# Three small edits in a decayed-attention and two-MLP kernel: two adds and a memset go from GpSimd to VectorE, and one set of sums of squares comes later

## The chip, the core and the metric

The kernel runs on one core of a Trainium2 chip. The core has five engines with in-order queues of their own: TensorE (PE, with weight loads shown as PEld), VectorE (DVE), ScalarE (ACT), GpSimd (POOL) and SyncE (SP, which here issues most DMAs). The metric is the device time of one launch in microseconds (us). Three runs of the kernel before took 890.89, 891.45 and 895.48 us; their median is 891.45 us.

## The reference

Three stages, in float32, on 4 sequences of 576 tokens with 8 heads of 64:

```python
scores = scale * q @ k.T                       # per head, 576 x 576
decay  = cum[:, :, :, None] - cum[:, :, None, :]   # cum = cumsum(log(clip(f)))
attn   = softmax(where(causal, -1e9, scores + decay))
x      = attn @ v                              # back to (4, 576, 512)
# first MLP, with LayerNorm and a residual
xn = (x - mean) / sqrt(var + 1e-6) * g_ln
x  = x + relu(xn @ w_ch1) @ w_ch2              # 512 -> 2048 -> 512
# gated MLP: h = relu(x @ w_in); u, v = halves; v is normalised over its features,
# mixed over the tokens by w_spatial, times u, then @ w_out
```

Two steps of it matter below: the variance of LayerNorm (a mean of squares over 512 features), and the softmax, whose rows are multiplied with v.

## The kernel before, in words

**Staging.** The attention is cut into eight blocks of query rows (`BLOCKS`): blocks 0 and 1 are rows 0 to 127 of two sequences each, blocks 2 and 3 rows 128 to 255 of two sequences each, blocks 4 to 7 rows 256 to 575 of one sequence each. What is left over of the last four (64 rows each) forms a ninth block of the first MLP. When a block's attention is done, its 256 tokens go through `norm`, and then form a group of the first MLP (`mlp`, 16 slices of the hidden layer). While PE works on the MLP of one group, the attention of a later block fills in: a table of due times in `run` (`SPAN`, `BEGIN`, and the constants `QKL`, `QKS`, `QKN` for `qknorm`) sets in which order the pieces are written, and a scheduler then orders each engine's queue from that.

**Arithmetic.** Products in full float32 are made from pairs of float16 halves: a high half made on ACT (`copy`, L304, or L669 for the weights) and a low half made on DVE (L388, L672). `make16` (L664 ff) makes the halves of the first MLP's weights once their scale is known.

**norm (L685 ff).** A tile x of 128 partitions by 4 x 256 tokens holds 512 features. PE takes the mean with a matrix of ones (L682); DVE subtracts it (L696); ACT squares (`sq`, L699); the four quarters of `sq` are folded to one by two adds on GpSimd (L703: 128 x 512, L704: 128 x 256); PE takes the mean of the result (L682 again); ACT and DVE make 1/sqrt of it (L707 to L711). Blocks 7 and 8 don't fold: PE sums the four quarters itself. So the fold occurs seven times, for blocks 0 to 6.

**GpSimd's other work.** For blocks 4 to 7 `operands` broadcasts rows of decays over the partitions (L338, a custom instruction, 96 times in all) and masks them (L342). In `weights` (L345 ff) a tile P of probabilities is cut into halves; for the last query tile, which has 64 columns less, its last columns are cleared by GpSimd (L382, 16 times) before P is transposed by DMA (L391) for the product with v (`values`, L533). P's buffers are a ring of five, so a clearing waits until the transposes of the same tile of the pair of heads before have been read out.

**qknorm (L260 ff).** q and k are scaled by powers of two that come from their sums of squares. Eight tiles of 896 KB are loaded through GpSimd's DMA queue (L277) into four buffers; for each, DVE sums the squares of q (L284) and ACT those of k (L285). The results set a scale (L290 to L297), then GpSimd scales the rows of decays and writes them to DRAM (L298, L299), where `operands` of block 4 reads them (L323).

Of the kernel before, what the change touches and what calls it, by code (L numbers as in the profile page):

```python
# [13 lines left out]
AF = mybir.ActivationFunctionType  # L14
ALU = mybir.AluOpType
# [21 lines left out]
NARROW = 4  # L37
# [29 lines left out]
F64_LO = 2.0 ** -15  # L67
VS = 10

QKL, QKS, QKN = 0.98, 1.2, 0.02  # L70
QKB = 4
MID = 416
CMAX = 2.0 ** 15
# [19 lines left out]
class Kernel:  # L93
# [166 lines left out]
    def qknorm(self):  # L260

        nc, W, C = self.nc, QW, QW + S
        n = B * NP // 2
        cm = self.pool("qs")
        qs = cm.__enter__()
        ss = self.cst.tile([P, 2, n], F32, name="qkss")
        tot = self.cst.tile([P, 2], F32, name="qkt")
        sm = self.qksc = self.cst.tile([P, 2, 2], F32, name="qksc")
        one = self.cst.tile([P, 1], F32, name="qkone")
        self.qkneg = self.cst.tile([P, 1], F32, name="qkneg")  # L270
        tiles = []

        def load():
            i = len(tiles)
            tiles.append(qs.tile([P, 2, C], F32, tag="qs", name="qs", bufs=QKB))
            b, p = i * 2 // NP, i * 2 % NP
            nc.gpsimd.dma_start(out=tiles[i], in_=self.pair_of(b)[p : p + 2].rearrange("p r s -> r p s"))  # L277

        for i in range(QKB):
            load()  # L280
        yield
        for i in range(n):
            q, k = tiles[i][:, :, :W], tiles[i][:, :, W:]
            nc.vector.tensor_tensor_reduce(out=q, in0=q, in1=q, scale=1.0, scalar=0.0, op0=ALU.mult, op1=ALU.add, accum_out=ss[:, 0, i : i + 1])  # L284
            nc.scalar.activation(k, k, AF.Square, accum_out=ss[:, 1, i : i + 1])  # L285
            if len(tiles) < n:
                load()
            yield
        nc.vector.tensor_reduce(out=tot, in_=ss, axis=mybir.AxisListType.X, op=ALU.add)
        pn = self.bank("s")  # L290
        nc.tensor.matmul(pn[:, :2], lhsT=self.ones, rhs=tot, start=True, stop=True)
        self.pow2(pn[:, :2], sm, up=3, k=0)
        uq, uk, sq, sk = (sm[:, i, j : j + 1] for i in range(2) for j in range(2))
        nc.vector.tensor_scalar(out=sk, in0=uq, scalar1=CMAX, scalar2=sk, op0=ALU.mult, op1=ALU.min)
        nc.vector.tensor_scalar(out=uk, in0=sq, scalar1=1.0 / CMAX, scalar2=uk, op0=ALU.mult, op1=ALU.max)
        nc.vector.tensor_scalar(out=one, in0=sq, scalar1=sk, scalar2=None, op0=ALU.mult)
        nc.vector.tensor_scalar(out=self.qkneg, in0=uq, scalar1=uk, scalar2=-0.125, op0=ALU.mult, op1=ALU.mult)  # L297
        nc.gpsimd.tensor_scalar(out=self.drow, in0=self.drow, scalar1=one[: B * H], scalar2=1.0, op0=ALU.mult, op1=ALU.mult)  # L298
        nc.gpsimd.dma_start(out=self.decay_d, in_=self.drow)  # L299
        cm.__exit__(None, None, None)  # L300
# [44 lines left out]
    def weights(self, i, heads):  # L345

        nc, at, bufs, q0 = self.nc, self.at, BUFS, 2 * P
        lo, hi = qtile(i)
        R, N, nb, qs = hi - lo, hi, i + 1, slice(lo - q0, hi - q0)
# [5 lines left out]
        for job in jobs:  # L355
            for g, (x, y) in enumerate(((xl, xh), (xh, xl), (xh, xh))):
                for u, n in job:
                    us, (c0, c1) = slice(64 * u, 64 * u + 64), cuts[n if R < P else 0]
                    out = banks[n][us if R < P else slice(0, P), : c1 - c0]
                    ins = nc.tensor.matmul(out, lhsT=x[us, qs], rhs=y[us, QW + c0 : QW + c1], start=g == 0, stop=g == 2, skip_group_check=True)  # L360
# [6 lines left out]
        for w in range(1 if R < P else 2):  # L367
            sd = at.tile([P, S], F32, tag="sd", name="sd", bufs=bufs["sd"])
            st = at.tile([P, 5], F32, tag="st", name="st", bufs=bufs["st"])
            for n, (c0, c1) in enumerate(cuts):  # L370
                self.marks["seen"] = nc.vector.tensor_tensor_reduce(  # L371
                    out=sd[:, c0:c1], in0=banks[n if R < P else w][:, : c1 - c0], in1=decay[i, w][:, c0:c1], scale=self.qkneg,
                    scalar=3e38 if n == 0 else st[:, n - 1 : n], op0=ALU.add, op1=ALU.min, accum_out=st[:, n : n + 1])
            n = len(cuts) - 1
            nc.scalar.activation(sd[:, :N], sd[:, :N], AF.Exp, bias=st[:, n : n + 1], scale=-1.0, accum_out=st[:, 2:3])  # L375
            rs = st[:, 3:4]
            nc.scalar.activation(rs, st[:, 2:3], AF.Copy, bias=1e-9 / SC, scale=1.0 / SC)  # L377
            nc.vector.reciprocal(rs, rs)  # L378
            ph = at.tile([P, 5, 2, P], F16, tag="P16", name="P16", bufs=bufs["P16"])
            pieces = [(0, i), (i, nb)] if R < P else [(0, nb)]  # L380
            if R < P:
                nc.gpsimd.memset(ph[:, i, :, R:], 0.0)  # L382
            for k0, k1 in pieces:
                wd = P if k1 * P <= N else R
                src = sd[:, k0 * P : k0 * P + (k1 - k0 - 1) * P + wd].rearrange("p (t w) -> p t w", w=wd)
                dh, dl = ph[:, k0:k1, 0, :wd], ph[:, k0:k1, 1, :wd]
                self.copy(0, dh, src, rs)
                low = nc.vector.scalar_tensor_tensor(out=dl, in0=src, scalar=rs, in1=dh, op0=ALU.mult, op1=ALU.subtract)  # L388
            for u in range(2) if R < P else [w]:
                rows = slice(R * u, R * u + R) if R < P else slice(0, P)  # L390
                tr = nc.sync.dma_start_transpose(out=heads[u][1][:, : 2 * nb, qs], in_=ph[rows, :nb].rearrange("p t h w -> p (t h w)"))  # L391
                self.in_order("tr", tr)
            if w == 0 and R == P:
                yield
# [269 lines left out]
    def make16(self, j):  # L664

        nc, src = self.nc, self.wt[:, j + 2]
        h, l = self.pair(j)
        for c, sc in ((slice(0, DM), self.w1c[:, 1]), (slice(DM, 2 * DM), self.w2c[:, 1])):
            ins = nc.scalar.activation(h[:, c], src[:, c], AF.Copy, scale=sc)  # L669
            if j >= SOON:  # L670
                self.after(ins, self.xh)
            nc.vector.scalar_tensor_tensor(out=l[:, c], in0=src[:, c], scalar=sc, in1=h[:, c], op0=ALU.mult, op1=ALU.subtract)  # L672

    def pair(self, j):
        w = self.wt[:, j].bitcast(F16)
# [6 lines left out]
            self.nc.tensor.matmul(pm, lhsT=self.onesf, rhs=x, start=i == 0, stop=i == len(xs) - 1)  # L682
        return pm

    def norm(self, x, s, y, whole, end, c):  # L685


        nc, ns = self.nc, self.ns
# [11 lines left out]
        if s is None or end:  # L700
            pv = self.mean(tag, *(sq[:, t] for t in range(NK)))
        else:
            nc.gpsimd.tensor_tensor(out=sq[:, :2], in0=sq[:, :2], in1=sq[:, 2:], op=ALU.add)  # L703
            nc.gpsimd.tensor_tensor(out=sq[:, 0], in0=sq[:, 0], in1=sq[:, 1], op=ALU.add)  # L704
            pv = self.mean(tag, sq[:, 0])
        t1 = ns.tile([P, TOK], F32, tag="t1", name="t1", bufs=2)
        nc.scalar.activation(y, pv, AF.Ln, bias=self.eps)  # L707
# [379 lines left out]
    def run(self):  # L1087
        self.setup()
        last = len(BLOCKS)
# [37 lines left out]
        def prep(n):  # L1127
# [22 lines left out]
            if g == 0:  # L1150
                self.y0 = y
            xc = tile() if n == 0 else xT
            g = self.norm(xT, s, y, g > 0, n >= last - 1, xc)
            while True:
                try:
                    with self.tc.high_priority(1):
# [169 lines left out]
```

## Time and profile before

| What | Value |
|---|---|
| median of three runs | 891.45 us (890.89 to 895.48) |
| the profiled execution: its time, its span | 894.41 us, 892.7 us |
| PE busy | 778.0 us (87% of the span) |
| DVE busy | 558.0 us (63%) |
| ACT busy | 513.0 us (57%) |
| POOL busy | 176.3 us (20%) |
| mean granted clock of TensorE | 0.933 of full speed |

The time of the profiled execution is that of the device; its span is what lies between the first and last instruction of the trace, here 1.7 us less. "Busy" counts instructions that work; an engine's idle time is put down to the event that ended it. A PE that is busy is not always at its full clock: the granted clock tells at which of its levels it ran.

### The profile page before, as it was taken

How to read it: one execution, taken by the hardware profiler on the slowest of the kernel's cores; microseconds unless marked ns; L12 is line 12 of the kernel's file. 1: busy time of each engine (PE TensorE's matmuls, PEld its weight loads, DVE VectorE, ACT ScalarE, POOL GpSimd, SP SyncE). 2: the span in 40 equal slices, each digit the busy share in tenths (PEclk: the TensorE clock that was granted, in tenths of full speed). 3: DMA queues.
4: the chain of work that ended last, by engine and by line, in shares of the span. 5: the costliest groups of instructions: out<-in, count | busy, mean ns of one | idle time of the engine just before them, and what ended most of it. 6: DMA issues, size and time to landing. Idle time of an engine off the chain costs nothing.

```text
span 892.7 us, 16774 instructions
## 1 busy us (share of the span) xinstructions
PE 778.0 (87%) x6108; PEld 574.9 (64%) x6108; DVE 558.0 (63%) x1481; ACT 513.0 (57%) x1294; POOL 176.3 (20%) x288
## 2 busy tenths in 40 slices
PE   8799988999647992899299749999999989999998
PEld 7588876877435771567187537784444757867776
DVE  4798599585536772877197728468843476273644
ACT  4878599584525762667176617446732583555643
POOL 2100011002526541534165223001002100000000
PEclk7999997999968997899699959999999989999999
DMA  8789794487414882577168707465203322010101
GB/s 249 220 307 332 237 300 78 73 168 124 121 45 98 145 164 48 96 138 162 28 120 174 127 19 108 96 200 144 93 1 65 73 66 76 1 55 1 47 8 54
DMA packets 162840, 103.99 MB, mean 116 GB/s; under 512 B 105955, under 2 KB 151139, under 8 KB 162757
## 3 DMA queue, kind: packets, MB, share of 16 engines
q1 hardware_dynamic: 155352, 88.91, 41.4%
q0 software_dynamic: 6400, 12.23, 6.7%
q10 hardware_dynamic: 1004, 1.78, 0.7%
q8 instruction: 48, 0.79, 0.4%
q14 instruction: 36, 0.29, 0.1%
HBM read 63.99 MB, written 14.72 MB: 88 GB/s over the span
## 4 chain that ended last, share of the span: by engine, by line
PE 47%; DVE 19%; issue 12%; ACT 10%; DMA 9%; POOL 3%; SPq 1%; POOLq 0%; DVEq 0%; ACTq 0%
PE ph L779 8%; PE acc L764 7%; PE pb L719 7%; PE pb L720 7%; PE pb L721 7%; DVE sd L371 3%; DMA PT<-P 2%; ACT sd L375 2%; DVE P L388 2%; ACT P L304 2%; DMA raw<-in_moe_w_ch_dram 2%; POOL D L338 2%; PE av L533 2%; DVE xql L328 2%; DVE hl L790 1%
## 5 line engine op out<-in xcount | busy, mean ns | idle before, releaser
L764 PE MATMUL acc<-hh,wt 128*128 128x256 f16 (+2 forms) x960 | 200.3, 298 | 4.3 <-DVE t L809 4.1
L779 PE MATMUL ph<-xh,wt 128*128 128x256 f16 (+1 forms) x896 | 192.0, 295 | 2.9 <-DVE hl L790 1.8
L779 PEld LDWEIGHTS <-wt 128*128 128x128 f16 x1344 | 132.0, 100 | 55.5 <-issue 16.3
L764 PEld LDWEIGHTS <-wt 128*128 128x128 f16 x1344 | 130.8, 99 | 53.6 <-issue 10.6
L779 PE MATMUL ph<-xl,wt 128*128 128x256 f16 (+1 forms) x448 | 132.2, 295 | 3.7 <-DVE xl L741 3.7
L764 PE MATMUL acc<-hl,wt 128*128 128x256 f16 (+1 forms) x416 | 117.4, 285 | 0.6 <-DVE hl L790 0.6
L338 POOL PARTITION_BROADCAST D<-row x96 | 81.9, 895 | 124.2 <-DVE st L371 66.7
L304 ACT ACTIVATE P<-sd,st 128x384 f16<-128x384 f32 (+2 forms) x128 | 70.0, 586 | 21.9 <-DVE st L378 16.0
L375 ACT ACTIVATE sd<-sd,st 128x384 f32<-128x384 f32 (+2 forms) x80 | 54.8, 685 | 46.7 <-DVE st L371 46.5
L786 ACT ACTIVATE hh<-ph 128x256 f16<-128x256 f32 (+2 forms) x128 | 50.7, 398 | 46.4 <-PE ph L779 46.1
L790 DVE SCALAR_TENSOR_TENSOR hl<-ph,hh 128x256 f16<-128x256 f32 (+1 forms) x112 | 50.6, 456 | 34.1 <-ACT hh L786 32.7
L682 PE MATMUL av<-sq,onesf 128*128 128x256 f32 x14 | 6.8, 578 | 74.5 <-POOL sq L704 74.5
L388 DVE SCALAR_TENSOR_TENSOR P<-sd,st,P 128x512 f16<-128x512 f32 (+1 forms) x96 | 60.3, 656 | 17.9 <-ACT P L304 16.8
L811 POOL DMA_DIRECT2D x_d<-t x36 | 33.6, 1116 | 147.0 <-DVE t L807 117.8
L378 DVE RECIPROCAL st<-st 128x1 f32<-128x1 f32 x80 | 11.7, 156 | 73.5 <-ACT st L377 73.5
L371 DVE CUSTOM_DVE_ANT_0 sd<-s,D,qkneg 128x384 f32<-128x384 f32 (+2 forms) x80 | 49.7, 644 | 12.6 <-PE s L360 12.1
L682 PEld LDWEIGHTS av<-sq,onesf 128*128 128x128 f32 x14 | 3.1, 258 | 76.1 <-POOL sq L704 76.0
L533 PE MATMUL av<-PT,vp 128*64 128x320 f16 (+2 forms) x480 | 35.8, 286 | 13.7 <-DMA PT<-P 13.2
L533 PEld LDWEIGHTS <-vp 128*64 128x64 f16 (+1 forms) x480 | 27.0, 115 | 24.1 <-issue 13.6
L719 PE MATMUL pb<-x2h,wil 128*128 128x288 f16 (+2 forms) x144 | 37.8, 273 | 0.0
L720 PE MATMUL pb<-x2l,wih 128*128 128x288 f16 (+2 forms) x144 | 37.8, 273 | 0.0
L721 PE MATMUL pb<-x2h,wih 128*128 128x288 f16 (+2 forms) x144 | 37.8, 273 | 0.0
(296 smaller groups left out, 1778.3 us busy)
## 6 DMA issues: line engine op xcount, KB each, us to landing
raw<-in_moe_w_ch_dram SPq DMA_DIRECT2D x32, 512.0 KB
qs<-in_qk_dram POOLq DMA_DIRECT2D x8, 896.0 KB, 9.2
qk<-in_qk_dram SPq DMA_DIRECT2D x16, 448.0 KB
vraw<-in_v_dram SPq DMA_DIRECT2D x5, 1024.0 KB
vr<-in_v_dram SPq DMA_DIRECT2D x16, 320.0 KB
x_d<-xT SPq DMA_DIRECT2D x9, 512.0 KB
x_d<-t POOLq DMA_DIRECT2D x36, 128.0 KB, 4.4
out_dram<-o SPq DMA_DIRECT2D x32, 144.0 KB
```

Of the source, the lines that this page charges most:

```text
L304: self.nc.scalar.activation(out, in_, AF.Copy, scale=scale)
L338: gp.partition_broadcast(t if R == P or u else t[:R], row[32 * u : 32 * u + 1, :hi], channels=P if R == P or u else R)
L371: self.marks["seen"] = nc.vector.tensor_tensor_reduce(out=sd[:, c0:c1], in0=banks[n if R < P else w][:, : c1 - c0], in1=decay[i, w][:, c0: ...
L375: nc.scalar.activation(sd[:, :N], sd[:, :N], AF.Exp, bias=st[:, n : n + 1], scale=-1.0, accum_out=st[:, 2:3])
L388: low = nc.vector.scalar_tensor_tensor(out=dl, in0=src, scalar=rs, in1=dh, op0=ALU.mult, op1=ALU.subtract)
L533: ins = nc.tensor.matmul(pav[us, n0:W], lhsT=vp[:kr, vi, kt, us], rhs=heads[u][1][:kr, 2 * kt + pi, n0:W], start=(kt == 0 and (vi, pi) == ...
L719: first = mm(out, lhsT=al, rhs=bh, start=start, stop=False, **kw)
L720: mm(out, lhsT=ah, rhs=bl, start=False, stop=False, **kw)
L721: mm(out, lhsT=ah, rhs=bh, start=False, stop=stop, **kw)
L764: ins = nc.tensor.matmul(acc[m], lhsT=a, rhs=b, start=bank not in clear, stop=last and e == len(terms) - 1, skip_group_check=True)
L779: ins = nc.tensor.matmul(ph, lhsT=a, rhs=b, start=k == e == 0, stop=k == NK - 1 and e == len(terms) - 1)
L790: nc.vector.scalar_tensor_tensor(out=hl, in0=ph, scalar=0.0, in1=hh, op0=ALU.max, op1=ALU.subtract)
```

## The change

Three edits:

1. `norm` gets an argument that names the engine of the fold. For blocks 0, 1 and 2 it stays GpSimd; for blocks 3 to 6 it is VectorE.
2. The clearing of P's last columns (`ph[:, i, :, R:]`) is done on VectorE.
3. `QKS`, the due time from which the sums of squares of q and k are written, goes from 1.2 to 1.325, and their spacing `QKN` from 0.02 to 0.008; both instructions of each tile are ordered behind the last low half that `make16` makes (`self.marks["made"]`). `after` gives an order of the schedule and no wait of its own.

```diff
-QKL, QKS, QKN = 0.98, 1.2, 0.02
+QKL, QKS, QKN = 0.98, 1.325, 0.008
...
-            nc.vector.tensor_tensor_reduce(out=q, in0=q, in1=q, ..., accum_out=ss[:, 0, i : i + 1])
-            nc.scalar.activation(k, k, AF.Square, accum_out=ss[:, 1, i : i + 1])
+            for ins in (nc.vector.tensor_tensor_reduce(out=q, in0=q, in1=q, ..., accum_out=ss[:, 0, i : i + 1]),
+                        nc.scalar.activation(k, k, AF.Square, accum_out=ss[:, 1, i : i + 1])):
+                self.after(ins, self.marks["made"])
...
-                nc.gpsimd.memset(ph[:, i, :, R:], 0.0)
+                nc.vector.memset(ph[:, i, :, R:], 0.0)
...
-            nc.vector.scalar_tensor_tensor(out=l[:, c], in0=src[:, c], scalar=sc, in1=h[:, c], ...)
+            self.marks["made"] = nc.vector.scalar_tensor_tensor(out=l[:, c], in0=src[:, c], scalar=sc, in1=h[:, c], ...)
...
-            nc.gpsimd.tensor_tensor(out=sq[:, :2], in0=sq[:, :2], in1=sq[:, 2:], op=ALU.add)
-            nc.gpsimd.tensor_tensor(out=sq[:, 0], in0=sq[:, 0], in1=sq[:, 1], op=ALU.add)
+            fold.tensor_tensor(out=sq[:, :2], in0=sq[:, :2], in1=sq[:, 2:], op=ALU.add)
+            fold.tensor_tensor(out=sq[:, 0], in0=sq[:, 0], in1=sq[:, 1], op=ALU.add)
...
-            g = self.norm(xT, s, y, g > 0, n >= last - 1, xc)
+            g = self.norm(xT, s, y, g > 0, n >= last - 1, xc, self.nc.gpsimd if n < NARROW - 1 else self.nc.vector)
```

How this moves instructions is shown at three places. From L282 on, line numbers of the changed kernel are higher by one.

On GpSimd, at the fold of block 4 (`sq` is the tile of squares, `D` the broadcast decays, `row` their source; an `ISA` without a tile asks for another set of GpSimd code). Before:

```order
L342 AFFINE_SELECT D_4064<-D_4064 64x64 x2
L703 ISA
L703 TENSOR_TENSOR sq_3615<-sq_3615 128x512
L338 ISA
L338 ISA D_4356<-row_4345 128x384
L338 ISA D_4354<-row_4345 128x384
L704 ISA
L704 TENSOR_TENSOR sq_3615<-sq_3615 128x256
L342 AFFINE_SELECT D_4356<-D_4356 128x128
L342 AFFINE_SELECT D_4354<-D_4354 128x128
L338 ISA
L338 ISA D_4366<-row_4345 128x512
```

and now:

```order
L343 AFFINE_SELECT D_4064<-D_4064 64x64 x2
L339 ISA D_4356<-row_4345 128x384
L339 ISA D_4354<-row_4345 128x384
L343 AFFINE_SELECT D_4356<-D_4356 128x128
L343 AFFINE_SELECT D_4354<-D_4354 128x128
```

The two adds, the clearing (which stood some rows further down) and the four changes of code around the adds are gone from GpSimd's queue; from the first broadcast on, only broadcasts, masks and DMAs stand there.

On VectorE, at the same place (`s` are scores in PSUM, `st` row statistics, `hl` a low half of the hidden layer, `P` the probabilities; `ISA` rows of L371 are the biased minimum and the read of its result). Before:

```order
L696 TENSOR_TENSOR xT<-xT,av 128x256 x4
L388 SCALAR_TENSOR_TENSOR P_3935<-sd,st,P_3935 128x4x128
L388 SCALAR_TENSOR_TENSOR P_3935<-sd,st,P_3935 128x64
L371 ISA sd,st<-s_3976,D,qkneg 128x384
L371 ISA st 128x1
L371 ISA sd,st<-s,D,qkneg 128x384
L371 ISA st 128x1
L790 SCALAR_TENSOR_TENSOR hl<-ph,hh 128x256
L378 RECIPROCAL st<-st 128x1 x2
L388 SCALAR_TENSOR_TENSOR P_3990<-sd,st,P_3990 128x3x128
```

and now:

```order
L697 TENSOR_TENSOR xT<-xT,av 128x256 x4
L389 SCALAR_TENSOR_TENSOR P_3935<-sd,st,P_3935 128x4x128
L372 ISA sd,st<-s_3976,D,qkneg 128x384
L372 ISA st 128x1
L389 SCALAR_TENSOR_TENSOR P_3935<-sd,st,P_3935 128x64
L372 ISA sd,st<-s,D,qkneg 128x384
L372 ISA st 128x1
L791 SCALAR_TENSOR_TENSOR hl<-ph,hh 128x256
L704 TENSOR_TENSOR sq<-sq 128x512
L379 RECIPROCAL st<-st 128x1
L705 TENSOR_TENSOR sq<-sq 128x256
L791 SCALAR_TENSOR_TENSOR hl<-ph,hh 128x256
```

Between the subtraction of the mean (L697) and the first add stand six rows of other work; the second add follows the first with one reciprocal in between.

On ScalarE, at the squares of k (`qs` is a loaded tile, `wt` the weights' halves, `hh` the ReLU of the MLP, `vp` halves of v). Before, first rows of the stretch:

```order
L669 ACTIVATE wt<-wt,w2c 128x512
L285 ACTIVATE qs,qkss<-qs 128x2x576
L217 ACTIVATE vp,vq<-vr 128x256
L699 ACTIVATE sq<-xT 128x1024
L285 ACTIVATE qs,qkss<-qs 128x2x576
L669 ACTIVATE wt<-wt,w1c 128x512
L669 ACTIVATE wt<-wt,w2c 128x512
L786 ACTIVATE hh<-ph 128x256
L285 ACTIVATE qs,qkss<-qs 128x2x576
```

and now:

```order
L670 ACTIVATE wt<-wt,w1c 128x512
L670 ACTIVATE wt<-wt,w2c 128x512
L507 ACTIVATE xT<-av,vs 128x128
L217 ACTIVATE vp,vq<-vr 128x256
L285 ACTIVATE qs,qkss<-qs 128x2x576 x4
L787 ACTIVATE hh<-ph 128x256
L488 ACTIVATE sd,st<-sd,st 128x256 x2
L787 ACTIVATE hh<-ph 128x256
```

The squares stood between the weights' halves; now four of them stand in one run behind the last of these halves, and the other four follow one at a time between the ReLUs and softmax pieces of blocks 2 and 3.

## Rows read from the trace of the kernel before

**Rows 1.** The page's 40 slices of 22.3 us, busy tenths of PE.
```profile
PE   8799988999647992899299749999999989999998
```

**Rows 2.** Waits of PE: for what, us in total, times, longest.
```profile
PE av L682 <- POOL sq L704: 74.5, 5, 20.8
PE av L533 <- DMA PT<-P: 13.2, 11, 4.0
```

**Rows 3.** PE in order of time: start, us, operation, [idle before, releaser].
```profile
258.35 1.22 PE L682 MATMUL av<-sq,onesf 128*128 128x256 f32 x2 [20.81 <-POOL sq L704]
...
356.54 1.22 PE L682 MATMUL av<-sq,onesf 128*128 128x256 f32 x2 [17.79 <-POOL sq L704]
...
442.98 1.22 PE L682 MATMUL av<-sq,onesf 128*128 128x256 f32 x2 [17.09 <-POOL sq L704]
...
526.03 1.22 PE L682 MATMUL av<-sq,onesf 128*128 128x256 f32 x2 [17.69 <-POOL sq L704]
```

**Rows 4.** Busy us by stretch: length, PE, PEld, DVE, ACT, POOL, clock, DMA, GB/s.
```profile
132.50:137.60 5.10, 1.01 (x19) 0.81 (x16) 5.10 (x15) 5.10 (x12) 0.01 (x1) 0.80 0.00 1
137.60:145.50 7.90, 7.89 (x41) 5.79 (x42) 7.90 (x23) 7.90 (x22) 3.62 (x4) 0.50 0.79 113
...
258.30:262.00 3.70, 3.65 (x16) 2.58 (x17) 1.57 (x4) 1.77 (x5) 0.00 (x0) 0.53 0.01 2
356.50:361.00 4.50, 4.46 (x19) 3.04 (x19) 1.67 (x4) 2.47 (x6) 0.50 (x2) 0.52 0.02 4
443.00:446.30 3.30, 3.30 (x14) 2.30 (x15) 0.92 (x2) 1.53 (x5) 0.43 (x2) 0.53 0.00 0
...
511.00:526.00 15.00, 0.00 (x0) 0.00 (x0) 0.34 (x1) 0.00 (x0) 2.07 (x5) 0.50 0.02 4
526.00:531.50 5.50, 5.47 (x25) 3.60 (x27) 1.25 (x3) 2.09 (x5) 0.48 (x2) 0.50 0.20 38
```

**Rows 5.** POOL in order of time, around the fold of block 4.
```profile
340.25 1.26 POOL L703 TENSOR_TENSOR sq<-sq 128x512 f32<-128x512 f32 x1 [7.93 <-DVE st L371]
347.31 1.23 POOL L338 PARTITION_BROADCAST D<-row  x2 [5.80 <-issue]
355.78 0.71 POOL L704 TENSOR_TENSOR sq<-sq 128x256 f32<-128x256 f32 x1 [7.24 <-issue]
...
362.88 1.95 POOL L338 PARTITION_BROADCAST D<-row  x2 [5.88 <-DVE st L371]
```

**Rows 6.** ACT in order of time, the squares of block 4.
```profile
334.14 1.06 ACT L699 ACTIVATE sq<-xT 128x1024 f32<-128x1024 f32 x1 [1.38 <-DVE xT L696]
```

**Rows 7.** DVE in order of time, during the fold of block 1.
```profile
110.83 0.75 DVE L672 SCALAR_TENSOR_TENSOR wt<-wt,w1c 128x512 f16<-128x512 f32 x1
111.49 1.77 DVE L672 SCALAR_TENSOR_TENSOR wt<-wt,w2c 128x512 f16<-128x512 f32 x1
```

**Rows 8.** POOL in order of time, the first add of block 1.
```profile
111.14 1.57 POOL L703 TENSOR_TENSOR sq<-sq 128x512 f32<-128x512 f32 x1 [0.31 <-ACT sq L699]
```

**Rows 9.** Groups of instructions by line: busy us, mean ns of one, idle before.
```profile
L285 ACT ACTIVATE qs<-qs 128x1152 f32<-128x1152 f32 x8 | 9.2, 1150 | 0.0
L284 DVE CUSTOM_DVE_ANT_1 qs<-qs 128x640 f32<-128x640 f32 x8 | 7.4, 919 | 0.0
...
L254 DVE TENSOR_TENSOR vtr<-vgram,ident 128x512 f32<-128x512 f32 x1 | 0.7, 683 | 0.0
```

**Rows 10.** Line L382, the clearing: ns min/median/max; its engine's idle time before it.
```profile
L382 POOL MEMSET P<- x16: 196/204/532, 265.9 to 560.0; 128x128 f16 x16
...
  DMA PT<-P: 8.6, 2
```

**Rows 11.** Line L277, the loads of q and k: time from issue to landing.
```profile
DMA to landing us min/median/max: 6.7/9.2/10.6
```

**Rows 12.** POOL in order of time, the write of the scaled decays.
```profile
204.93 0.84 POOL L299 DMA_DIRECT2D decay_d<-drow  x1
```

**Rows 13.** SP's queue in order of time, block 4's first reads of the decays.
```profile
220.37 0.73 SPq L323 DMA_DIRECT2D row<-decay_d  x2
```

More of the change, by code (lines that the diff above doesn't have):

```diff
@@ L283, in qknorm @@
             q, k = tiles[i][:, :, :W], tiles[i][:, :, W:]
-            nc.vector.tensor_tensor_reduce(out=q, in0=q, in1=q, scale=1.0, scalar=0.0, op0=ALU.mult, op1=ALU.add, accum_out=ss[:, 0, i : i + 1])
-            nc.scalar.activation(k, k, AF.Square, accum_out=ss[:, 1, i : i + 1])
+            for ins in (nc.vector.tensor_tensor_reduce(out=q, in0=q, in1=q, scale=1.0, scalar=0.0, op0=ALU.mult, op1=ALU.add, accum_out=ss[:, 0, i : i + 1]),
+                        nc.scalar.activation(k, k, AF.Square, accum_out=ss[:, 1, i : i + 1])):
+                self.after(ins, self.marks["made"])
             if len(tiles) < n:
@@ L671, in make16 @@
                 self.after(ins, self.xh)
-            nc.vector.scalar_tensor_tensor(out=l[:, c], in0=src[:, c], scalar=sc, in1=h[:, c], op0=ALU.mult, op1=ALU.subtract)
+            self.marks["made"] = nc.vector.scalar_tensor_tensor(out=l[:, c], in0=src[:, c], scalar=sc, in1=h[:, c], op0=ALU.mult, op1=ALU.subtract)
     def pair(self, j):
@@ L683, in mean, with norm @@
         return pm
-    def norm(self, x, s, y, whole, end, c):
+    def norm(self, x, s, y, whole, end, c, fold):
         nc, ns = self.nc, self.ns
```

## The prediction

> **What bounds the kernel now.** I read four views, from coarse to fine. First the page's slices: PE works at 9 tenths nearly everywhere, but slices 11, 15, 19 and 23 (counted from 0) show 4, 2, 2 and 4 [rows 1]. Four holes at a distance of some 85 us, which is one block of attention: something happens once per block. Then the waits of PE: 74.5 us of idle time are put down to one line, the second mean of `norm`, released by GpSimd's second add of the fold; the next largest wait, on transposes of P, is 13.2 us in eleven pieces [rows 2]. The timeline of PE gives the four large ones, at blocks 3 to 6: 20.81, 17.79, 17.09 and 17.69 us, together 73.4 us [rows 3]. Third, what the other engines do then: in 511 to 526 PE and ACT do nothing, DVE 0.34 us, the DMA engines are at 0.02, and GpSimd itself is busy for only 2.07 of 15 us [rows 4]. So nothing is prefetched or caught up on in a hole; the whole kernel stands still, and it stands for something that is not even GpSimd's work.
>
> What that is, GpSimd's timeline tells. At block 4 the squares were ready at 334.14 + 1.06 = 335.2 [rows 6], PE came to the mean at 356.54 - 17.79 = 338.75 [rows 3]. The first add started at 340.25; between it and the second GpSimd did two broadcasts, and in front of each of these pieces it sat 5.8 to 7.2 us with no releaser but "issue" [rows 5]. The adds and the broadcasts alternate, and each alternation is where the order shows a bare `ISA` row, a change of GpSimd's code. The adds themselves take 1.26 and 0.71 us; three changes of some 5 to 7 us each make up the 21 us from the squares to the folded tile. A fourth change, back to the broadcasts, costs another 5.88 us before 362.88 [rows 5], when PE already runs again.
>
> **The change, part by part. The fold.** It removes from GpSimd the two adds of blocks 3 to 6 and with them all sixteen changes of code; the four waits of 73.4 us lose their cause [rows 3]. It adds the same two adds to DVE. No 128x512 add of two SBUF tiles on DVE stands in the trace, but one from PSUM and SBUF does: 0.68 us [rows 9]; the second is half as long, and I take 0.4. What is late next? At block 4 the squares come at 335.2, and PE needs the fold at 338.75: 3.55 us of cover. In DVE's new order a ReLU low half, and perhaps the last of two score passes, stand ahead of the first add and a reciprocal between the adds; that leaves the fold done 2 to 4 us after the squares, so PE waits 0 to 0.5 us, and I put 2 us in all for the four blocks. Upper bound: 5 us for each, 20 us, if the add always comes behind a full pass of scores and low halves. Gain 71.4.
>
> A word against it. While GpSimd's first add ran from 111.14 to 112.71 [rows 8], a two-input DVE instruction of L672 that takes 0.75 us took 1.77 [rows 7]: the two engines slowed each other. The Trainium skill ("GPSIMD Engine Reference", section 1, Specifications) says that GpSimd shares its SBUF interfaces with VectorE and that DVE instructions with two SBUF inputs contend there. The moved adds have two SBUF inputs, and broadcasts run beside them all the time; by this rule each pair of adds would cost some 1.5 us more, an estimate, 6 us in four blocks. By the rows alone it is 0 to that, as no broadcast beside an add on DVE is seen, and the bound of 20 us holds it.
>
> **The clock.** After each hole PE runs at half of its full clock: the granted clock is 0.50 to 0.53, which is the 1.2 GHz level, in the four stretches behind them, with 3.65, 4.46, 3.30 and 5.47 us of PE work [rows 4], 16.9 us in all. At the 2.4 GHz level that is 8.4 us. PE stood idle before each of these stretches and would not any more. Some of it is work that ran ahead of DVE and ACT catching up; I take 6, with 0 and 8.4 as bounds.
>
> **The clearing.** Sixteen memsets of 0.2 us leave GpSimd [rows 10]; on DVE I take 0.1 us each, 1.6 us of an engine that is 63% busy, hidden by PE's work. It now carries a wait in DVE's queue: for the transposes of the same tile one pair of heads before. Behind it stand the low halves of P of the third query tile and the next scores, for whose transposes PE waits. On GpSimd this wait showed in 2 of 16 cases, 8.6 us together [rows 10]. But `values` on PE waits for the same transposes at about the same time [rows 2], so most of a hold is time that PE doesn't have anyway. I take a loss of 1, bounds 0 and 8.6.
>
> **The squares of q and k.** 8 x 0.92 = 7.4 us of DVE and 8 x 1.15 = 9.2 us of ACT [rows 9] leave the stretch from 103 to 140, where both engines are busy all the time: 5.10 of 5.10 us, while PE works 1.01 [rows 4]. There PE waits 4.1 us for the output copies of group 0, which stand behind squares and weights' halves in DVE's queue; then follow 7.89 us at clock 0.50 [rows 4], 3.9 us lost by that. Ideal gain 8; since ACT and DVE still have the halves to make, I take 4. The bill comes later: four squares in one run hold ACT for 4 x 1.15 = 4.6 us in front of a ReLU that PE needs two hidden slices later, and the last four need loads that go out only when a buffer is free and land 6.7 to 10.6 us later [rows 11]. In between lies about as much other ACT work. I take a loss of 2, bounds 0 and 10. Two queues are moved past: on GpSimd the loads now stand behind the output adds of group 0, and the scaled decays are written behind the four output adds of group 1, some 3.5 us later than at 204.93 [rows 12]; their reader starts at 220.37 [rows 13], 15 us after, and covers it. So net gain 2, bounds -10 and +8.
>
> **The sum.** 73.4 - 2 + 6 - 1 + 4 - 2 = 78.4 us. The profiled execution took 894.4 us (its span 892.7 and 1.7 around it): 816.0. It was 3.0 us above the median of the three runs, so the median after should be 891.45 - 78.4 = 813.
>
> **The rivals.** *The wait moves to DVE (A).* The fold now stands in the queue of an engine that is full in the attention of these blocks, and each mean still waits 5 us; the clock then drops all the same. Gain 73.4 - 20 + 2 = 55: 836. For it: an in-order queue with score passes of two at a time. Against: the order puts the adds early, and 3.55 us of cover. *More comes back (B).* The broadcasts that came late after a hole made `values` wait for transposes: the longest such wait, 4.0 us, and much of the 13.2 [rows 2], would go as well, with the whole of the clock's 8.4 and 8 for the squares: 73.4 + 8.4 + 8 + 5 = 95: 797. *The squares collide (C).* ACT holds for each late load, PE's ReLU is behind it: the loss is 10 and the gain there 0: 73.4 - 2 + 6 - 1 - 10 = 66: 825. *Slower (D).* The clearing holds DVE each time until the transposes are out, as it did on GpSimd twice. If each of 16 took 8.6 us, that is 138 us: 813 + 138 = 951; from 78.4 / 16 = 4.9 us each on the change loses. Against: 14 of 16 had no wait [rows 10] on an engine that comes to them no later than DVE will. *It doesn't do what it says (E).* Other GpSimd work could still ask for the old code between the broadcasts, and the holes would stay: 890. Against: the new order has no bare `ISA` row after the first, and masks and clearings ran between broadcasts without one before.
>
> **How the numbers follow.** Forecast 0.70, A 0.11, B 0.08, C 0.07, D 0.02, E 0.02. The forecast's own range is 803 to 825. The range that should hold 8 in 10 reaches to B below and to A above: 799 to 836. A change below 0.5% (4.5 us) can't be told from none here: faster 0.96, same 0.02, slower 0.02.
>
> **What would show it.** Right: no wait of PE on GpSimd's adds beyond the first microseconds of the kernel; no slices of 2 to 4 before the end of the attention; the mean's matmuls released by DVE with waits below 1 us; clock near 1.0 through the blocks; GpSimd without idle "issue" pieces of 6 us; the squares behind the last weights' halves and PE's wait near 133 shorter. Wrong: waits of some 5 us at the four means on DVE (A); ACT idle for a load near 155 to 165 (C); DVE idle for transposes ahead of memsets (D); the four holes still there (E).

## The result: 816 us, and the profile after

The changed kernel takes 815.71 us (median of 4 runs, 812.2 to 817.82), the kernel before beside it 891.17: a ratio of 0.914, 95% interval 0.9094 to 0.9186. In a second set of runs, reported at the end of the experiments, the ratio was 0.9157 (0.9132 to 0.9181). The profiled execution took 812.2 us, its span 810.5; it is the fastest of its four, as that of before was near its slowest, so the two spans differ by 82.2 us and the medians by 75.5. One execution of a kernel further down, the one without the squares, took 979.22 us at a mean granted clock of 0.747, where its six others took 813.7 to 819.3, and nothing is read from it.

The page's slices, PE's busy tenths, against [rows 1]:

```profile
PE   8799998997899899899899989999999899999998
```

The four slices of 2 and 4 are gone; what is left below 8 is a 7 in slices 1 and 9. PE is busy 764.6 us instead of 778.0 and idle 45.9 instead of 114.7. The waits of PE (what for, us in total, times, longest), against [rows 2]:

```profile
PE av L534 <- DMA PT<-P: 9.9, 11, 2.1
PE ph L780 <- DVE hl L791: 8.9, 8, 1.7
PE s L481 <- DMA qk<-decay_d: 2.4, 1, 2.4
PE ph L780 <- ACT xh L741: 2.0, 1, 2.0
```

The 74.5 us on GpSimd's second add have become 1.1, one wait in the first microseconds. The four matmuls of the mean at blocks 3 to 6, in order of time (start, us, operation, [idle before, releaser]), against [rows 3]:

```profile
230.19 0.60 PE L683 MATMUL av<-sq,onesf 128*128 128x256 f32 x2
310.62 0.60 PE L683 MATMUL av<-sq,onesf 128*128 128x256 f32 x2
375.37 0.60 PE L683 MATMUL av<-sq,onesf 128*128 128x256 f32 x2
438.55 0.67 PE L683 MATMUL av<-sq,onesf 128*128 128x256 f32 x2 [0.55 <-ACT st L378]
```

Three of them wait for nothing, and the fourth 0.55 us for something else than the fold. A pair takes 0.60 us where it took 1.22: the clock. Stretches behind these four means, as long as those of [rows 4] (length, PE, PEld, DVE, ACT, POOL, granted clock, DMA share, GB/s):

```profile
230.20:234.20 4.00, 4.00 (x40) 3.13 (x39) 3.40 (x7) 3.03 (x8) 3.78 (x9) 1.00 0.24 63
310.60:315.10 4.50, 4.50 (x45) 3.57 (x44) 2.87 (x10) 3.56 (x11) 2.07 (x4) 1.00 0.66 114
375.30:378.60 3.30, 3.30 (x34) 2.69 (x33) 2.44 (x7) 2.42 (x8) 1.88 (x3) 1.00 1.13 107
438.50:444.00 5.50, 5.45 (x48) 4.43 (x48) 5.21 (x15) 4.75 (x12) 1.75 (x4) 1.00 0.47 87
```

All at 1.00, the 2.4 GHz level. GpSimd around the fold of block 4, which is [rows 5] with the adds gone:

```profile
301.02 2.29 POOL L339 PARTITION_BROADCAST D<-row  x2 [4.10 <-DVE st L372]
303.39 0.79 POOL L343 TENSOR_SCALAR_AFFINE_SELECT D<-D 64x64 f32<-64x64 f32 x2
306.86 1.40 POOL L339 PARTITION_BROADCAST D<-row  x2 [2.68 <-DVE st L372]
308.33 0.94 POOL L343 TENSOR_SCALAR_AFFINE_SELECT D<-D 128x128 f32<-128x128 f32 x2
```

No piece of idle "issue" stands between them; GpSimd waits for buffers that VectorE gives free. A change of code (a bare `ISA` row of the order) stands in the trace as two records named MODIFY_POOL_CONFIG. At the line of the broadcasts there were 18 in the kernel before, two changes to the broadcasts' code for each of the four folds and one ahead of the first broadcast, and 8 at each line of the adds; in the changed kernel only the first pair is left (ns min/median/max, first and last start):

```profile
L338 POOLq MODIFY_POOL_CONFIG  x18: 1/1/358, 209.2 to 526.7; - x18
...
L339 POOLq MODIFY_POOL_CONFIG  x2: 42/42/42, 206.8 to 206.8; - x2
```

On ScalarE and VectorE the same fold reads (two adds of later blocks below it):

```profile
305.59 1.06 ACT L700 ACTIVATE sq<-xT 128x1024 f32<-128x1024 f32 x1
```

```profile
307.69 0.98 DVE L704 TENSOR_TENSOR sq<-sq 128x512 f32<-128x512 f32 x1
308.70 0.42 DVE L705 TENSOR_TENSOR sq<-sq 128x256 f32<-128x256 f32 x1
...
373.06 0.68 DVE L704 TENSOR_TENSOR sq<-sq 128x512 f32<-128x512 f32 x1
...
436.90 0.71 DVE L704 TENSOR_TENSOR sq<-sq 128x512 f32<-128x512 f32 x1
```

From the end of the squares (306.65) to the folded tile (309.12) it is 2.5 us, where it was 21. And line L383, the clearing, now on VectorE (ns min/median/max, first and last start; its engine's idle time before it), against [rows 10]:

```profile
L383 DVE MEMSET P<- x16: 112/112/112, 235.8 to 486.3; 128x64 uint32 x16
...
  DMA PT<-P: 1.0, 3
```

### The profile page after: what moved, and what is told of

Read it like the earlier page. It is cut to its first block, busy times and chain, and to the rows that moved or that the text cites. A ratio compares the mean times of both kernels' runs of the same rounds, so it can differ in the third digit from the quotient of the medians.

```text
span 810.5 us, 16721 instructions
## 1 busy us (share of the span) xinstructions
PE 764.6 (94%) x6108; PEld 568.1 (70%) x6108; DVE 561.8 (69%) x1505; ACT 509.7 (63%) x1294; POOL 174.1 (21%) x264
## 4 chain that ended last, share of the span: by engine, by line
PE 65%; DVE 15%; DMA 8%; ACT 7%; issue 4%; SPq 1%; DVEq 0%; ACTq 0%
PE ph L780 15%; PE acc L765 13%; PE pb L720 7%; PE pb L721 7%; PE pb L722 7%; DMA PT<-P 4%; PE av L534 3%; PE s L765 3%; DVE sd L372 2%; DVE xql L329 2%; ACT P L305 2%; DVE P L389 2%; ACT sd L376 1%; PE s L361 1%; DVE vp L226 1%
## 5 line engine op out<-in xcount | busy, mean ns | idle before, releaser
L765 PE MATMUL acc<-hh,wt 128*128 128x256 f16 (+2 forms) x960 | 197.3, 296 | 1.7 <-DVE t L808 1.4
L780 PE MATMUL ph<-xh,wt 128*128 128x256 f16 (+1 forms) x896 | 186.5, 290 | 11.0 <-DVE hl L791 8.9
L780 PEld LDWEIGHTS <-wt 128*128 128x128 f16 x1344 | 129.6, 99 | 61.9 <-issue 25.5
L765 PEld LDWEIGHTS <-wt 128*128 128x128 f16 x1344 | 129.6, 98 | 47.1 <-issue 8.6
L780 PE MATMUL ph<-xl,wt 128*128 128x256 f16 (+1 forms) x448 | 130.0, 290 | 0.0
L339 POOL PARTITION_BROADCAST D<-row x96 | 84.1, 917 | 116.0 <-DVE st L372 95.6
L534 PE MATMUL av<-PT,vp 128*64 128x320 f16 (+2 forms) x480 | 33.3, 270 | 9.9 <-DMA PT<-P 9.9
L1063 DVE SCALAR_TENSOR_TENSOR u<-pb,wsc,u 128x288 f32<-128x288 f32 x32 | 15.9, 515 | 34.3 <-PE pb L1062 34.3
L343 POOL TENSOR_SCALAR_AFFINE_SELECT D<-D 128x128 f32<-128x128 f32 (+1 forms) x96 | 36.8, 397 | 4.7
L534 PEld LDWEIGHTS <-vp 128*64 128x64 f16 (+1 forms) x480 | 24.7, 109 | 17.7 <-issue 8.4
L720 PE MATMUL pb<-wsh,vl 128*128 128x288 f16 x128 | 36.6, 286 | 0.4 <-DVE x2s L206 0.2
```

The lines of the kernel that those rows point to most:

```text
L339: gp.partition_broadcast(t if R == P or u else t[:R], row[32 * u : 32 * u + 1, :hi], channels=P if R == P or u else R)
L534: ins = nc.tensor.matmul(pav[us, n0:W], lhsT=vp[:kr, vi, kt, us], rhs=heads[u][1][:kr, 2 * kt + pi, n0:W], start=(kt == 0 and (vi, pi) == ...
L720: first = mm(out, lhsT=al, rhs=bh, start=start, stop=False, **kw)
L765: ins = nc.tensor.matmul(acc[m], lhsT=a, rhs=b, start=bank not in clear, stop=last and e == len(terms) - 1, skip_group_check=True)
L780: ins = nc.tensor.matmul(ph, lhsT=a, rhs=b, start=k == e == 0, stop=k == NK - 1 and e == len(terms) - 1)
```

## The experiments

The theory after this result: one cause, the change of GpSimd's code between an add and a broadcast, made the holes; taking away all of them is the gain. Rivals: the adds were slow on GpSimd and fast on VectorE; the squares' move, which brought the first output copy of group 0 from 136.8 to 126.5, carries part of the gain. Each ratio is to the kernel before on the same chip.

**Each edit alone.** The fold alone on VectorE:

```diff
# kernel before, with:
-            nc.gpsimd.tensor_tensor(out=sq[:, :2], ...)
-            nc.gpsimd.tensor_tensor(out=sq[:, 0], ...)
+            fold.tensor_tensor(out=sq[:, :2], ...)     # fold: VectorE from block 3 on
+            fold.tensor_tensor(out=sq[:, 0], ...)
```

> The kernel before with the fold of blocks 3 to 6 on VectorE alone; the clearing stays on GpSimd and the squares of q and k stay between the weights' halves. Theory (the holes are GpSimd's changes of code between its adds and its broadcasts, and this edit takes all sixteen away): 891.2 - 73.4 + 2 - 6 = 814 by the terms of the prediction, 812 to 820; the four waits on GpSimd's second add are gone, with the stretches at half clock behind them. Rival 1 (the squares carry some 10 us of the gain, as group 0's output copies end 10 us earlier in the changed kernel): 824 to 828. Rival 2 (the clearing costs on VectorE what it waits for): below 812, faster than the changed kernel.

Measured: 812.98 us, ratio 0.9102 (0.9067 to 0.9137). It lies in the theory's 812 to 820, and the fold alone gives at least what all three edits give together. Rival 1 (824 to 828) falls; rival 2 (below 812) is missed by 1 us and comes back at the end.

The clearing alone:

```diff
# kernel before, with:
-                nc.gpsimd.memset(ph[:, i, :, R:], 0.0)
+                nc.vector.memset(ph[:, i, :, R:], 0.0)
```

> The kernel before with the clearing of P's last columns on VectorE alone. Theory: no more than 1 us either way, 890 to 893, as the four holes stay and the memsets lie under PE's work. Rival 1 (GpSimd's broadcasts come earlier once it no longer waits 8.6 us for transposes of P): 880 to 887. Rival 2 (VectorE is held for the transposes instead, and scores and low halves stand behind): 895 to 900.

Measured: 891.42 us, ratio 0.9992 (0.9973 to 1.0011): nothing that can be told, 2.4 us less to 1.0 us more. Both rivals fall.

The squares of q and k alone:

```diff
# kernel before, with:
-QKL, QKS, QKN = 0.98, 1.2, 0.02
+QKL, QKS, QKN = 0.98, 1.325, 0.008
...
+                self.after(ins, self.marks["made"])    # both squares of a tile
...
+            self.marks["made"] = nc.vector.scalar_tensor_tensor(out=l[:, c], ...)
```

> The kernel before with the sums of squares of q and k behind the weights' halves alone. Theory (10 us are gained by 126, and most of it is lost again to late loads before 222, as in the changed kernel): 888 to 890, a gain of 1 to 3. Rival 1 (the whole 10 us stay): 880 to 883. Rival 2 (what is gained is lost, and more): 893 to 897.

Measured: 898.85 us, ratio 1.0071 (1.0043 to 1.0098). Slower, by 3.8 to 8.7 us: the theory missed, and rival 2's sign holds, at a price beyond its own. New or longer waits of PE in this kernel:

```profile
PE ph L780 <- DVE hl L791: 7.9, 7, 1.5
PE s L481 <- DMA qk<-decay_d: 2.6, 1, 2.6
PE ph L780 <- ACT xh L741: 2.1, 1, 2.1
```

The 4.1 us for the output copies of group 0 are gone, as the prediction had it, and so are most of 3.7 us on low halves of x. But low halves of the hidden layer now cost 7.9 instead of 1.8 us, a load of block 3 costs 2.6 us that were not there, and the high half of x 2.1 instead of 1.0. The same three waits stand in the changed kernel's list above.

Fold and clearing together, without the squares (the two diffs above):

> The changed kernel without the move of the squares: fold and clearing on VectorE, squares of q and k between the weights' halves. Theory: 816 to 819, 1 to 3 above the changed kernel. Rival 1 (the squares' 10 us stay): 824 to 827. Rival 2 (the squares' move costs as much as it brings): 813 to 816. Beside the run with the fold alone it shows the clearing: within 1 of it by the theory, 3 to 8 above it if VectorE is held for transposes.

Measured: 817.47 us, ratio 0.915 (0.9117 to 0.9184), in the theory's bounds. Rival 1 (824 to 827) falls; rival 2's 813 to 816 cannot be told from the theory, since the interval reaches from 813.5 to 819.5. The sign that was named for a clearing that holds VectorE, 3 to 8 us above the fold alone, came out by its number: 4.5 us above 812.98 on the same chip, with intervals that overlap. But in this kernel the trace shows no idle time of VectorE in front of the sixteen memsets, so a hold is not what made it.

Fold and squares, with the clearing left on GpSimd:

> The changed kernel with the clearing left on GpSimd: fold on VectorE and squares of q and k behind the weights' halves. Theory (the clearing and the squares' place each move the time by less than 4 once the holes are gone, by the order that comes of them): 811 to 817. Rival 1 (the clearing on VectorE costs some 4, as the two kernels with it were at 815.7 and 817.5 and the one without at 813.0): 809 to 813. Rival 2 (the squares' place costs 6, as it did with the holes): 818 to 821.

Measured: 816.3 us, ratio 0.9128 (0.9101 to 0.9154), again as the theory has it. Rival 1 (809 to 813) falls, since the kernel without the clearing's move is no faster than the one with all three edits, and so does rival 2 (818 to 821).

**Is it the change of code?** The changed kernel, with two adds of 128x1 per block put on GpSimd that nobody reads:

```diff
# changed kernel, in norm, with:
+            if fold is nc.vector:
+                tiny = ns.tile([P, 1], F32, tag="tiny", name="tiny", bufs=2)
+                nc.gpsimd.tensor_tensor(out=tiny, in0=sq[:, 2, :1], in1=sq[:, 3, :1], op=ALU.add)
+                nc.gpsimd.tensor_tensor(out=tiny, in0=tiny, in1=sq[:, 3, :1], op=ALU.add)
             pv = self.mean(tag, sq[:, 0])
```

> The changed kernel with two adds of 128x1 put on GpSimd behind the squares of each of the blocks 3 to 6, of results that nobody reads; the fold itself stays on VectorE. GpSimd so has the kind of instruction back, without its work and without a reader. Theory (GpSimd loads other code each time an add follows a broadcast and the reverse): idle pieces of 5.5 to 7.5 us come back in front of the adds and of the broadcasts behind them, 14 of them, though each add takes 0.1 us; the means don't wait, but the broadcasts of the next decays come 10 to 20 us later, and 816 becomes 818 to 832. Rival 1 (the adds themselves, 1.26 and 0.71 us, and GpSimd's long queue made the hole): no idle pieces, 814 to 818. Rival 2 (late broadcasts hold the scores as much as the late fold held the mean): 860 to 890.

Measured: 862.06 us, ratio 0.9633 (0.9606 to 0.9659). Some 46 us of the gain are gone again (42 to 44 by the ratios), by eight instructions of 0.2 to 1.1 us. GpSimd around the squares of block 4, in order of time, and the changes of code:

```profile
338.93 0.18 POOL L708 TENSOR_TENSOR tiny<-sq 128x1 f32<-128x1 f32 x1 [8.63 <-ACT sd L376]
344.86 0.95 POOL L339 PARTITION_BROADCAST D<-row  x1 [5.76 <-DVE xql L329]
353.10 0.18 POOL L709 TENSOR_TENSOR tiny<-tiny,sq 128x1 f32<-128x1 f32 x1 [7.28 <-issue]
359.01 0.68 POOL L339 PARTITION_BROADCAST D<-row  x1 [5.73 <-issue]
...
L339 POOLq MODIFY_POOL_CONFIG  x16: 1/2/42, 208.7 to 507.8; - x16
```

The idle pieces of [rows 5] are back, as long as there, around instructions with hardly any work; with 16 records at the line of the broadcasts and 8 and 6 at the tiny adds there are 14 changes of code more than in the changed kernel, as many as the theory counted (at block 5 the two adds stand together). So the first rival (slow adds) is out. But the price is above the theory's 2 to 16 us: no mean of these blocks waits longer than 0.5 us here, and still PE stands. Its four longest waits, in order of time:

```profile
250.00 0.50 PE L361 MATMUL s<-xqh,xql 64*128 64x384 f16 x2 [8.38 <-DVE st L372]
...
272.73 0.42 PE L534 MATMUL av<-PT,vp 128*64 128x320 f16 x1 [11.03 <-DMA PT<-P]
...
368.00 0.48 PE L534 MATMUL av<-PT,vp 128*64 128x320 f16 x1 [13.88 <-DMA PT<-P]
...
439.34 0.45 PE L534 MATMUL av<-PT,vp 128*64 128x320 f16 x1 [4.26 <-DMA PT<-P]
```

Together 37.6 us. The first is plain: scores need the broadcast decays. The others wait for transposes of P, and SP's queue tells why, here at block 4 (start, us, DMA; then the queue's waits, us in total, times, longest):

```profile
330.59 0.54 SPq L324 DMA_DIRECT2D row<-decay_d  x2
333.08 10.76 SPq L392 DMA_TRANSPOSE PT<-P  x6
344.63 0.37 SPq L320 DMA_DIRECT2D qk<-in_qk_dram  x1
364.29 0.51 SPq L324 DMA_DIRECT2D row<-decay_d  x2
364.90 2.54 SPq L392 DMA_TRANSPOSE PT<-P  x2
```

```profile
SPq L324 <- POOL D L339: 60.5, 11, 19.2
```

From 345.0 to 364.29 SP stands at the read of the next row of decays, whose buffer the late broadcasts still hold, and two transposes of P stand behind it. In the changed kernel this wait is 13.1 us in 11 pieces, the longest 3.2; in the kernel before it was 39.3 in 10, the longest 18.0. VectorE is held as well, by the clearing that the change gave it (28.5 us in six pieces; the longest):

```profile
369.32 0.11 DVE L383 MEMSET P<- 128x64 uint32 x1 [12.64 <-DMA PT<-P]
```

The remaining 9 us are the clock. In three stretches with these waits (the columns as above) it is below 1.00:

```profile
223.00:260.00 37.00, 27.45 (x213) 19.77 (x212) 24.48 (x60) 19.27 (x50) 13.22 (x25) 0.82 0.39 100
...
368.00:400.00 32.00, 30.09 (x276) 22.85 (x277) 21.89 (x59) 19.07 (x51) 15.77 (x26) 0.90 0.83 157
430.00:470.00 40.00, 31.98 (x303) 24.62 (x303) 27.95 (x70) 21.98 (x59) 20.20 (x34) 0.96 0.72 141
```

PE's work times what is missing to 1: 27.45 x 0.18 + 30.09 x 0.10 + 31.98 x 0.04 = 9.2 us, and 37.6 + 9.2 = 46.8. So rival 2's number is right, at the low end of its 860 to 890, and its mechanism in part: 8.4 us are scores that wait for late broadcasts, the larger part are transposes behind SP's queue. That second chain is what the theory was short of. How much of it there would be with the clearing on GpSimd, so that VectorE is not held, was not tested.

The control has masks in the place of the tiny adds, a kind that already stands between the broadcasts:

```diff
# kernel with the tiny adds, with:
-                nc.gpsimd.tensor_tensor(out=tiny, in0=..., in1=..., op=ALU.add)
+                nc.gpsimd.affine_select(out=tiny, in_=sq[:, 2, :1], pattern=[[1, 1]], ...)   # and sq[:, 3, :1]
```

> As the kernel with two tiny adds on GpSimd in each of the blocks 3 to 6 (862.1), but the tiny instructions are masks of 128x1, a kind that already stands between the broadcasts; they wait for the same squares and nobody reads them. Theory (what cost 46 us is the change of code between an add and a broadcast, not the instruction's place in GpSimd's queue or its wait for the squares): no idle pieces of 6 us around them, 814 to 819. Rival (the broadcasts are late because GpSimd's queue waits at these places for ScalarE's squares): 830 to 862.

Measured: 815.5 us, ratio 0.9148 (0.9124 to 0.9172), the changed kernel's own time. GpSimd at block 4:

```profile
306.08 0.19 POOL L708 TENSOR_SCALAR_AFFINE_SELECT tiny<-sq 128x1 f32<-128x1 f32 x1 [2.77 <-ACT sq L700]
306.23 0.67 POOL L339 PARTITION_BROADCAST D<-row  x1
306.75 0.29 POOL L709 TENSOR_SCALAR_AFFINE_SELECT tiny<-sq 128x1 f32<-128x1 f32 x1
307.14 1.07 POOL L339 PARTITION_BROADCAST D<-row  x1
```

Same place, same size, a wait for the squares, and no idle piece on "issue"; the line of the broadcasts has the first pair of records and no other. So what cost 46 us is the kind of instruction, a TENSOR_TENSOR among broadcasts, and not its place or its wait. The Trainium skill ("GPSIMD Engine Reference", section 2.1, Instruction dispatch) says that the first call of freshly loaded GpSimd code pays a load of about 6 us that no instruction in the profile shows. The pieces of 5.7 to 7.5 us with the tiny adds are of that size or somewhat longer; that it is paid anew at each alternation is what these runs add.

**One hole by itself.** The changed kernel with the fold of block 4 alone back on GpSimd:

```diff
# changed kernel, with:
-self.nc.gpsimd if n < NARROW - 1 else self.nc.vector
+self.nc.gpsimd if n < NARROW - 1 or n == 4 else self.nc.vector
```

> The changed kernel with the fold of block 4 alone back on GpSimd. Theory (each hole is paid by itself): one hole of 17 to 18 us before the second mean, some 4.5 us of PE at 0.52 behind it (2.1 us): 816 + 18 + 2 = 836, 832 to 840. Rival 1 (the holes help each other, and PE makes a single one up later): 818 to 828. Rival 2 (a hole costs more than its wait, as broadcasts behind it come late as well): 841 to 848.

Measured: 835.11 us, ratio 0.9331 (0.9301 to 0.9361): 19.4 us above the changed kernel's 815.7, or 15.5 to 17 by the ratios to the kernel before. It is the theory's 832 to 840; both rivals' ranges are missed. The mean of block 4 and the stretch behind it:

```profile
329.12 1.22 PE L683 MATMUL av<-sq,onesf 128*128 128x256 f32 x2 [17.48 <-POOL sq L705]
```

```profile
329.10:333.60 4.50, 4.48 (x25) 3.16 (x27) 1.22 (x4) 2.20 (x5) 0.48 (x2) 0.62 0.02 4
```

17.48 us of waiting and 4.48 x 0.38 = 1.7 us of clock make 19.2. A hole is paid once, in full as far as the scatter lets one tell, and little is made up later. Its broadcasts came late as well (GpSimd stood 6.03 and 5.92 us before two of them), but PE has no further wait for transposes above 2.1 us. SP came to its next read of a row only at 341.51, behind the hole, and at such reads it stands 10.9 us in ten pieces here, the longest 2.7: what late broadcasts hold lies in the time of the mean's wait. That is why rival 2 fell here, and its number holds above.

**What the squares could bring at most.** The fold on VectorE, and the sixteen squares of q and k left out, their sums set to 1:

```diff
# kernel with the fold alone, with:
-            nc.vector.tensor_tensor_reduce(out=q, ...)
-            nc.scalar.activation(k, k, AF.Square, ...)
+            if i == 0:
+                nc.vector.memset(ss, 1.0)
```

> The kernel before with the fold of blocks 3 to 6 on VectorE, and with the sixteen instructions of the squares of q and k left out (their sums are set to 1; the loads stay). It is the most that any place for them can bring beside the fold alone (813.0). Theory (what is gained before 140 is mostly lost again by 220, as the next block's loads and not the weights' halves set the pace there): 808 to 813. Rival 1 (VectorE and ScalarE bound the stretch, and the gain lasts): 798 to 806.

Measured: 817.73 us, ratio 0.9135 (0.9104 to 0.9165). Not one of the 16.6 us of work on two engines comes back; theory (808 to 813) and rival (798 to 806) both expected less time than that. The same kernel again:

> The kernel with the fold on VectorE and the sixteen squares of q and k left out, for a profile at full clock. Theory (the attention of block 2 sets the pace up to 220: its last values release, through the write of its x, the reads of the next block on SP; its transposes of P and values don't wait for the squares): its last values come between 172 and 175 as with the squares between the halves (174.5), though group 0's output copies end near 125, and the time is 812 to 818. Rival (without squares the attention ends early too, and the time is lost later by another order): last values before 168.

Measured: 816.24 us, ratio 0.9146 (0.9116 to 0.9176). The time is in the theory's 812 to 818. The last value of block 2's attention in this kernel, a little ahead of the theory's 172, then in the changed one:

```profile
171.75 0.37 ACT L506 ACTIVATE xT<-av,vs 128x128 f32<-128x128 f32 x1 [2.00 <-PE av L505]
```

```profile
175.60 0.37 ACT L507 ACTIVATE xT<-av,vs 128x128 f32<-128x128 f32 x1 [1.06 <-PE av L506]
```

Right behind it SP writes this x (at 175.99 in the changed kernel) and only then issues the reads of block 3, so this instant releases the next block. Moving the squares does not bring it forward: it was 175.49 before and is 175.40 with them moved; with the fold on VectorE it is 174.46 without the move and 175.60 with it. Even leaving them out brings only 2.7 us against 174.46. The guess that group 0's output copies would then end near 125 missed; they start at 138.5 to 139.5. So the copies are early in the changed kernel by the order that the scheduler makes of the later squares, not by the engines' free time.

What PE gained at the copies it loses behind that instant. Two stretches of the changed kernel, then the second of them in the kernel before (the columns as above):

```profile
132.00:146.00 14.00, 11.56 (x101) 9.27 (x101) 14.00 (x38) 13.67 (x35) 0.00 (x0) 0.88 0.44 82
190.00:205.00 15.00, 9.35 (x63) 6.21 (x62) 13.45 (x51) 11.81 (x41) 3.82 (x5) 0.58 0.91 136
...
190.00:205.00 15.00, 13.88 (x128) 10.76 (x128) 14.30 (x55) 14.83 (x52) 1.41 (x3) 1.00 0.69 112
```

The stretch behind the copies, at 0.50 in [rows 4] and 0.63 from 132 to 146, is at 0.88 now. But from 190 to 205, where PE worked 13.88 us at 1.00, it works 9.35 at 0.58, and the waits of 2.4 us for a load and of 2.0 for x lie there. 9.35 x 0.42 = 3.9 us: as much as the half clock behind the copies had cost. In the main the half clock was moved, not removed.

**Does the fold alone beat the changed kernel?** Both again, on one chip, with no edit but those above.

> The changed kernel again, on one chip with the kernel that has the fold alone on VectorE. Theory (clearing and squares' place are worth nothing that can be measured, and may cost some us): 814 to 818, a ratio to before of 0.912 to 0.917, 0 to 4 above the fold alone. Rival (they bring what the prediction gave them, 1 us): 1 below the fold alone.

> The fold alone on VectorE, again, beside the changed kernel. Theory: 811 to 815, a ratio of 0.909 to 0.913; if its interval lies below that of the changed kernel, it beats both. Rival: 816 to 818, no difference.

Measured: 816.34 us, ratio 0.9157 (0.9132 to 0.9181), and 814.42 us, ratio 0.9131 (0.911 to 0.9152). The fold alone is lower both times, by 2.7 us (not beside each other) and 1.9 (on one chip), but the intervals overlap. Whether the other two edits cost 2 us or nothing stays open; that they bring no gain that can be told is shown.

## Why the prediction was right, and where not

The forecast was 813, and 815.7 was measured. Step by step:

- **The four waits, 73.4 us, and what is left of them, 2.** Right. They fell to 0.55 us. The cause is the one named, changes of GpSimd's code: the tiny adds bring the idle pieces back, the masks don't.
- **The clock, 6 of 0 to 8.4.** Right in kind; the rows say 8.1, the medians don't decide. The four stretches are at 1.00 now. At the full level the work in [rows 4], with the clocks beside it, would have been shorter by 3.65 x 0.47 + 4.46 x 0.48 + 3.30 x 0.47 + 5.47 x 0.50 = 8.1 us; PE works through the four stretches all but without a pause, so nothing had to be held back for VectorE and ScalarE catching up. By these two steps (73.4 - 0.5 and 8.1) the fold alone should give 72.9 + 8.1 = 81.0; the profiled spans differ by 892.7 - 810.9 = 81.8. But the profiled execution of the kernel before was 2 to 3 us above its medians (894.41 against 892.27 and 891.17), and against those of the fold alone they differ by 79.3 and 77.8, which 72.9 + 6 = 78.9 fits as well.
- **The clearing, -1 of 0 to -8.6.** Right in size. Alone it moves the time by -0.7 us (-2.4 to +1.0), and in the changed kernel VectorE waits 1.0 us in all at it. The 4.5 us between the fold alone and fold with clearing stand against that by their number, but without a wait at the memset in the trace, and the other pair (816.3 without the clearing's move, 815.7 and 816.3 with it) doesn't show them. Rival D's mechanism is real, though: with the broadcasts late, one memset held VectorE 12.64 us. It is harmless only as long as the transposes come in time.
- **The squares, +4 and -2.** Wrong, and the step that failed is the first: that a stretch in which VectorE and ScalarE are busy all the time gives back time if work is taken out of it. It took the wait for the output copies, and the half clock behind it, as the price of the squares. The wait did go, but the release of the next block is the end of block 2's attention, and that did not come earlier. PE ran ahead with MLP work and had that much less to do from 190 to 205, where it waits for a load and x instead, at a clock of 0.58. Alone the edit costs 3.8 to 8.7 us; in the changed kernel it is lost in the measurement (815.7 and 816.3 with it, 817.5 without it). The bound of -10 held it. That the sum came within 3 us in spite of it is owed to the size of the term, +2, and is no support for its mechanism; the fold's part, 71.4 + 6 = 77.4 against 77.8 and 79.3 measured, carries the hit.
- **Rival A** (the wait moves to VectorE) fell: no mean waits for VectorE. **Rival B** (late broadcasts) named the right second mechanism and put it at 5 us. The transposes' wait fell from 13.2 to 9.9 us, so in the sum it is 3. The kernel with the tiny adds shows what it is worth alone; in the kernel before, its wait and the mean's lay in the same time. **Rival C** (ScalarE holds for late loads of q and k) fell: ScalarE waits 0.6 us for them, in two pieces. **Rival D** (VectorE held for 138 us) and **rival E** (other work asks for the old code) fell with the 1.0 us at the memsets and the one change of code that is left. D's price took the sum of two waits, 0.53 and 8.07 us, for one; by the longer it would have been 129 us.
- **The contention.** The eight adds take 5.4 us, 1.1 more than by the prediction's 0.68 and 0.4, and PE waits for none of them. The longest ran beside broadcasts: a 128x512 add took 0.98 us at 307.69, with a broadcast until 308.26, against 0.68 at 373.06, where the broadcast ended at 373.20, and a 128x256 add 0.88 at 228.23. But two others had broadcasts beside them as well and took 0.71 (128x512, at 436.90) and 0.54 (128x256, at 437.86). The rule of the Trainium skill ("GPSIMD Engine Reference", section 1, Specifications) on interfaces shared with VectorE fits the long ones and is not borne out by the short ones; the estimate of 6 us from it was too high for adds beside broadcasts.

What the prediction had only in rival B, and at 5 us: the holes had two chains with one cause. The fold was late for PE, and the broadcasts were late for SP's queue and so for the transposes. With the fold taken away and two adds of one column per block left on GpSimd, 32 us came of it (893.8 to 862.1 on one chip) instead of 76.

## What to carry to other kernels

Where an engine changes code between two kinds of instruction, count the alternations in its order, not the work: one small instruction of the wrong kind costs the engine the same idle time as the large one. Before taking a wait away, follow everything else that the late engine releases, queues included; a second chain in the same time does not show in the waits of the engine that bounds the kernel until the first is gone. And a stretch where two engines are full is worth emptying only if what releases the next stretch is in it.

## What the runs showed of the hardware that was not expected

- A change of code costs the same in front of a small instruction as of a large one: GpSimd stood 7.28 us in front of an add of 0.18 us at block 4 with the tiny adds, and 7.24 in front of one of 0.71 us in [rows 5]; in front of broadcasts it stood 5.73 and 5.80. A mask after an add needs none, as the mask behind the second add of block 4 shows: it starts at 356.46 in the kernel before, as the add ends (355.78 + 0.71).
- SP's queue, when it waits for a buffer, holds what stands behind it: two transposes of P stood up to 19.2 us behind a read of a row of decays.
- The clearing of 128x128 f16 (the trace has it as 128x64 uint32 on VectorE, the same bytes) takes 0.112 us on VectorE, each time; on GpSimd it was 0.20 in the median [rows 10].
